# A gated attention and mixer kernel: where the last two chunks of the first z are loaded

## The chip, the cores and the metric

The kernel runs on one core of a Trainium2 chip. The metric is the device time of one execution, in microseconds (us). Seven inputs are read from HBM, one output is written to it; the time covers all of that.

The core's engines each run their own list of instructions in order: TensorE (PE in the profile, PEld for its weight loads), VectorE (DVE), ScalarE (ACT), GpSimd (POOL) and SyncE (SP). An instruction that has to wait for another engine or for a DMA holds up all that stands behind it on its own engine. SyncE, ScalarE and GpSimd can issue DMAs, each on a queue of its own (q1, q10 and q0 in the profile).

## The reference

Batch 8, sequence S = 3008, width D = 256, z of width 64, all float32. First a gated attention, then an MLP mixer on what it gives:

```python
scores = scale * np.matmul(z, z.transpose(0, 2, 1))      # scale = 1 / S
attn = np.maximum(scores, 0.0) ** 2
x = u * np.matmul(attn, v)
# mixer, for each batch
xt = x.transpose(0, 2, 1)
h = np.maximum(xt @ w_tok1, 0.0) @ w_tok2                # over the sequence, 256 channels
u = x + h.transpose(0, 2, 1)
h2 = np.maximum(u @ w_ch1, 0.0) @ w_ch2                  # over the width, 1536 channels
out = u + h2
```

The scores of a batch are a product of z with itself, so z is needed transposed (width on the partitions), both as weights and as the moving side.

## The kernel before

The sequence is cut in six chunks of 512 rows (the last has 448); a chunk is four tiles of 128 rows. For each batch the kernel goes over six blocks of queries (one chunk each), and within a block over the six chunks of keys. For a pair of chunks TensorE makes scores in two units (two key tiles each, line 440), ScalarE applies the ReLU and the scale (line 478), VectorE squares (line 486), and TensorE multiplies with v and accumulates (line 593 in the very first block, line 677 in the others). VectorE then multiplies with the transposed u (line 835). When a batch's blocks are done, its mixer is mixed in between the attention of the following batch.

Nearly everything is ordered at build time. The code carries a small planner: it holds an estimate of when each engine is free, when each tile is ready, and what each step costs, and picks the next piece for TensorE from that (`while cur[0] is not None or heads or tails`). The order so found is then fixed in each engine's list of instructions. On the chip, semaphores decide when each instruction really starts. An estimated due time therefore changes the order, not the waiting.

The start of the program is written out by hand, and the change is in it. The z of batch 0 isn't transposed like the others':

- `first_z(c)` loads chunk c of the first z in float32 into a tile `zf` (line 162). Chunk 5 has three full tiles and a half one; the half one is filled by two more loads of the same 64 last rows (line 165), to both halves of the partitions. Even chunks go over SyncE's queue, odd ones over ScalarE's, and the two loads of last rows one over each.
- `double_first_z(c)` has VectorE cast a chunk to bfloat16 and write it twice side by side (line 171), as `zr`.
- `turn_on_pe` transposes it on TensorE against an identity matrix (line 177); a copy moves the result to `zT` (by ScalarE, line 1639, for chunks 0 and 1; by VectorE, line 1643, for chunk 3, and line 1573 for chunks 4 and 5). Chunk 2 alone is transposed by a DMA on SyncE's queue (`turn_first_z`, line 149).
- Chunks 4 and 5 are handled by `late_z(c, landed)`: it asks the planner for a cast on VectorE at the time `landed`, an urgent piece on TensorE when that cast is done, and a copy on VectorE behind it.

Around this, GpSimd issues the first chunk of v at once (line 211, `load_v(0, 0)`). Its other five chunks of the first v, and then u, come behind `after(...)`, a small copy that waits for ScalarE's copy of chunk 1's transpose. TensorE begins with seven filler products (line 198) and fills up to the first product with v with five more. The tile pool gives VectorE's `zr` and GpSimd's v their buffers.

In the first block the keys are taken in the order 0, 1, 3, 2, 4, 5, so the scores of chunks 4 and 5 are made last.

The wait of the casts, on VectorE, is on the semaphores of the loads: the cast of chunk 5 waits for its own load and for both loads of last rows. On VectorE the squares that follow stand behind such a cast.

Of the kernel before, what the change touches and what calls it, by code (L numbers as in the profile page):

```python
# [15 lines left out]
GK = 4  # L16
# [41 lines left out]
def kernel(  # L58
# [11 lines left out]
    nc = tc.nc  # L70
# [11 lines left out]
    NG = KT // GK  # L82
# [30 lines left out]
    def rows_of(ap, c):  # L113

        n = full_tiles[c]
        return ap[c * QW:c * QW + n * P, :].rearrange("(p t) d -> p t d", t=n)

    def last_rows(ap):
        return ap[(KT - 1) * P:, :]
# [27 lines left out]
    def turn_first_z(c):  # L147

        nc.sync.dma_start_transpose(
            out=zTs[0][:, c * GK:c * GK + GK, :],  # L150
            in_=double_first_z(c).rearrange("p t h d -> p (t h d)"))
# [5 lines left out]
    def first_z(c):  # L157

        zf = sb.tile([P, GK, d_qk], F32, tag="v", name="zf", bufs=ROOM["v"])
        n = full_tiles[c]  # L160
        queues = [nc.sync, nc.scalar]
        queues[c % 2].dma_start(out=zf[:, :n, :], in_=rows_of(z[0], c))
        if n < GK:
            for r in range(2):
                queues[r].dma_start(
                    out=zf[r * TAIL:(r + 1) * TAIL, n, :], in_=last_rows(z[0]))
        return zf

    def double_first_z(c):
        zr = sb.tile([P, GK, 2, d_qk], BF16, tag="xT", name="zr0", bufs=ROOM["xT"])  # L170
        nc.vector.tensor_copy(zr[:], zf0[c].unsqueeze(2).to_broadcast([P, GK, 2, d_qk]))
        return zr

    def turn_on_pe(zr, zp):

        for t in range(GK):
            nc.tensor.matmul(  # L177
                zp[:, t, :], zr[:, t].rearrange("p h d -> p (h d)"), ident[:],
                start=(t == 0), stop=True, skip_group_check=True)

    def bank_pair(slot, name):

        if slot == RING and not last_psum:
            first.close()
            last_psum.append(ctx.enter_context(
                tc.tile_pool(name="last_psum", bufs=1, space=bass.MemoryType.PSUM)))
        pool = psum if slot < RING else last_psum[0]
        return pool.tile([P, 2, QW], F32, tag=f"ps{slot}", name=name, bufs=1)
# [12 lines left out]
    def load_v(b, c):  # L201
        if b == 0:

            vt = sb.tile([P, GK, D], BF16, tag="fl", name="v_sb", bufs=ROOM["fl"])
            live["fl"] += 1
            fl_free.pop(0)
        else:
            vt = sb.tile([P, GK, D], BF16, tag="v", name="v_sb", bufs=ROOM["v"])
            live["v"] += 1
        n = full_tiles[c]  # L210
        nc.gpsimd.dma_start(out=vt[:, :n, :], in_=rows_of(v[b], c))
        if n < GK:
            for r in range(2):
                nc.gpsimd.dma_start(
                    out=vt[r * TAIL:(r + 1) * TAIL, n, :], in_=last_rows(v[b]))
        vs[b, c] = vt
        v_in[b, c] = Done(pe[0] + 9.0 if b > 1 else 0.0)
        loading(LOAD)
# [120 lines left out]
    def push(engine, ready, busy, lat, fn, first=0, room=(), done=None, frees=()):  # L339
        op = Op(ready, busy, lat, fn, first, room, done, frees)  # L340
        waiting[engine].append(op)
        return op.done
# [80 lines left out]
    def score_run(us, start):  # L423
        for unit in us:
            (b, q, g), pr = unit
            zT = zTs[b].rearrange("p t s -> p (t s)")
            W = widths[q]
            slot, free_at = take_slot()
            begin = max(start, free_at, known(turned[b, q], turned[b, g]))
            cost = column_time(W)  # L430
            if triangle(b, q, g):

                cost = (column_time(QW), column_time(P))[pr]
            begin, start = on_pe(begin, "half", cost)
            sc = bank_pair(slot, "sc")
            for r, i, c0, c1 in parts(unit):
                k = z_tile(b, r, g * GK + i) * P
                m = z_tile(b, r, q * GK) * P
                h = slice(r * d_qk, (r + 1) * d_qk)
                nc.tensor.matmul(  # L440
                    sc[:, r, c0:c1], zT[h, k:k + P], zT[h, m + c0:m + c1],
                    start=True, stop=True)
            if pr == 0:
                live["at"] += 1
                at_free.pop(0)
            busy = 0.92
            if triangle(b, q, g):
                busy = (0.87, 0.43)[pr]
            if grain(b, q, g) < GK and pr == 0:
                early[b, q, g] = [Done() for _ in range(GK)]  # L450
            done = push("act", begin + cost + 0.21, busy, busy + 0.16,
                        lambda t, unit=unit, sc=sc: relu(unit, sc, t))
            ring.append((done, slot))
# [424 lines left out]
    def take_slot():  # L878
        slot = min((s for s in ring if s[0].t is not None), key=lambda s: s[0].t)
        ring.remove(slot)  # L880
        return slot[1], slot[0].t
# [576 lines left out]
    zero = sb.tile([P, QW], BF16, tag="xT", name="zero", bufs=ROOM["xT"])  # L1458
    nc.vector.memset(zero[:], 0.0)
    make_identity(nc, ident)  # L1460
    zf0 = [first_z(c) for c in range(NG)]
    load_v(0, 0)
    nc.gpsimd.memset(zs[:, 0, :], 0.0)
    nc.gpsimd.memset(zs[:, KT + 1, :], 0.0)
# [96 lines left out]
    def late_z(c, landed):  # L1561


        zr = []

        def turn(end):
            slot, _ = take_slot()
            zp = bank_pair(slot, "zp")[:, 0, :].rearrange("p (t s) -> p t s", s=P)
            turn_on_pe(zr[0], zp)
            turned[0, c] = Done()  # L1570
            ring.append((push(
                "dve", end + 0.2, 0.66, 0.8,
                lambda t: nc.vector.tensor_copy(zTs[0][:, c * GK:c * GK + GK, :], zp),
                first=1, done=turned[0, c]), slot))

        cast = push("dve", landed, 0.42, 0.55, lambda t: zr.append(double_first_z(c)))
        heads.append(Piece(0.23, [cast], turn, urgent=True))


    def first_u(landed):  # L1580

        ur = urs.pop((0, 0))

        def turn(end):
            slot, _ = take_slot()
            up = bank_pair(slot, "up").rearrange("p r (t s) -> p (r t) s", s=P)
            for i in range(QW // P * DT):
                t, h = divmod(i, DT)
                nc.tensor.matmul(  # L1589
                    up[:, i, :], ur[:, t, h * P:(h + 1) * P], ident[:],  # L1590
                    start=(i % 4 == 0), stop=True, skip_group_check=True)
            ring.append((push("dve", end + 0.2, 1.15, 1.3, lambda t: evacuate(up)), slot))

        def evacuate(up):
            uTs[0, 0] = sb.tile([P, QW // P, DT, P], BF16, tag="uT", name="uT", bufs=3)
            nc.vector.tensor_copy(
                uTs[0, 0].rearrange("p t h s -> p (t h) s"), up)

        heads.append(Piece(0.45, [Done(landed)], turn, urgent=True))
# [36 lines left out]
    for c in range(DT):  # L1636
        zp = first_acc(c).rearrange("p (t s) -> p t s", s=P)
        turn_on_pe(double_first_z(c), zp)
        nc.scalar.copy(zTs[0][:, c * GK:c * GK + GK, :], zp)
    turn_first_z(2)  # L1640
    zp = bank_pair(2, "zp")[:, 0, :].rearrange("p (t s) -> p t s", s=P)
    turn_on_pe(double_first_z(3), zp)
    nc.vector.tensor_copy(zTs[0][:, 3 * GK:4 * GK, :], zp)
# [8 lines left out]
    pe[0] = 5.3  # L1652
    free.update(act=5.75, dve=5.0, sp=7.0)
    score_run(units[:2], 5.3)
    late_z(4, 7.8)
    late_z(5, 9.0)
    first_u(18.5)

    goals = {(1, 1): (0, 1 + HALF)}
# [147 lines left out]
```

## Time and profile before

| | us |
|---|---|
| median of 3 runs (1116.61 to 1116.9) | 1116.72 |
| the profiled execution: its time | 1117.16 |
| its span, first to last instruction | 1115.0 |
| TensorE busy in the span | 1104.5 |
| VectorE busy | 761.9 |
| ScalarE busy | 673.0 |
| GpSimd busy | 152.2 |
| TensorE busy from 8.70 to 30 us (21.30) | 21.09 |
| TensorE busy from 30 to 60 us (30.00) | 30.00 |
| ScalarE busy from 30 to 60 us (30.00) | 28.97 |

The granted clock of TensorE is 0.999 of full speed. The times of a trace are counted from its first instruction. A busy TensorE isn't TensorE at its peak, since the ends of pipelined products are modelled; that it never stands idle in a stretch is read from the waits and from the chain. The chain of waits is followed back from the last instruction: at each step to what released it, or to the instruction before it on its engine. A line of a DMA gives its tiles, the queue that issued it, its size and the time from issue to landing. In a timeline the columns are start, duration, engine, line, operation and tiles; "x3" merges three that follow each other, and the bracket behind tells how long the engine was idle before, and what ended that.

### The profile page before, as it was taken

The numbers are of one execution on the slowest core, as the hardware profiler recorded it, in microseconds if no ns is written. First come the engines' busy times: TensorE is split into PE (matmuls) and PEld (weight loads), VectorE is DVE, ScalarE is ACT, GpSimd is POOL, SyncE is SP. The second block draws the span as 40 slices with busy tenths as digits, with TensorE's granted clock in tenths as the row PEclk, the third lists the DMA queues.
The fourth block names the chain that finished last, engine by engine and source line by source line (L and its number), as shares of the span: only waits on it lengthen the run. The fifth ranks groups of instructions, "written<-read, shape, count | busy, mean of one in ns | idle before, by whom it ended". The sixth has DMA issues, their size and how long they took to land.

```text
span 1115.0 us, 26448 instructions
## 1 busy us (share of the span) xinstructions
PE 1104.5 (99%) x10714; PEld 666.6 (60%) x10788; DVE 761.9 (68%) x1587; ACT 673.0 (60%) x840; POOL 152.2 (14%) x387
## 2 busy tenths in 40 slices
PE   9999999999999999999999999999999999999998
PEld 3555654666447665676545765567654576545676
DVE  7887875676756867568656676566756677655676
ACT  8997585545755467555665456664666636743464
POOL 5401000221002210022100221003210021000000
PEclk9999999999999999999999999999999999999999
DMA  9999485997859988598694997869888697574222
GB/s 173 189 167 185 105 165 110 189 172 145 165 117 193 168 132 183 95 210 168 139 179 96 204 155 153 164 104 219 141 156 153 127 200 145 120 153 84 66 65 80
DMA packets 470411, 165.38 MB, mean 148 GB/s; under 512 B 433232, under 2 KB 448912, under 8 KB 470288
## 3 DMA queue, kind: packets, MB, share of 16 engines
q1 hardware_dynamic: 442432, 130.98, 59.2%
q0 software_dynamic: 27344, 32.32, 20.7%
q8 instruction: 84, 1.38, 0.5%
q14 instruction: 39, 0.32, 0.1%
q10 hardware_dynamic: 512, 0.38, 0.1%
HBM read 65.40 MB, written 24.64 MB: 81 GB/s over the span
## 4 chain that ended last, share of the span: by engine, by line
PE 98%; DMA 1%; issue 0%; POOL 0%; DVE 0%; ACT 0%; POOLq 0%
PE acc L677 42%; PE hp L977 22%; PE f L1096 18%; PE sc L440 6%; PE a_ps L900 4%; PE h_ps L927 4%; PE f L1209 1%; PE first_acc L593 1%; DMA v_sb<-in_v_dram 1%; PE op L1255 0%; PE zp L177 0%; PE up L1589 0%; DVE res L1287 0%; ACT a_sb L909 0%; POOL ident masks.py:199 0%
## 5 line engine op out<-in xcount | busy, mean ns | idle before, releaser
L1024 ACT ACTIVATE h2pre<-hp 128x1024 bf16<-128x1024 f32 (+1 forms) x287 | 283.3, 1005 | 226.6 <-PE hp L977 217.3
L677 PEld LDWEIGHTS <-v_sb 64*128 64x128 bf16 x4418 | 231.2, 94 | 227.8 <-issue 0.9
L677 PE MATMUL acc<-at,v_sb 64*128 64x512 bf16 (+1 forms) x2738 | 337.7, 374 | 0.0
L478 ACT ACTIVATE at<-sc 128x1024 bf16<-128x1024 f32 (+1 forms) x290 | 285.6, 1029 | 69.3 <-PE sc L440 64.1
L486 DVE TENSOR_TENSOR at<-at 128x1024 bf16<-128x1024 bf16 (+1 forms) x290 | 198.0, 686 | 123.5 <-ACT at L478 121.5
L977 PE MATMUL hp<-xT,w_ch_sb 128*128 128x512 bf16 (+1 forms) x1090 | 278.4, 374 | 3.3
L1096 PEld LDWEIGHTS <-h2pre 128*128 128x128 bf16 x3654 | 225.0, 98 | 55.3 <-issue 2.6
L677 PE MATMUL acc<-fl,v_sb 64*128 64x512 bf16 (+1 forms) x1680 | 191.8, 367 | 0.0
L1096 PE MATMUL f<-w_sums,h2pre 128*128 128x128 bf16 x2088 | 184.4, 219 | 0.1
L977 PEld LDWEIGHTS <-w_ch_sb 128*128 128x128 bf16 x1152 | 104.3, 98 | 82.1 <-issue 0.8
L440 PE MATMUL sc<-zT 64*128 64x512 bf16 (+1 forms) x732 | 131.3, 359 | 0.0
L1096 PE MATMUL f<-w_ch_sb,h2pre 128*128 128x128 bf16 x1566 | 128.5, 219 | 0.0
L811 DVE TENSOR_TENSOR cp<-acc,cp 128x512 f32<-128x512 f32 (+1 forms) x94 | 63.5, 675 | 57.1 <-ACT cp L805 56.3
L805 ACT COPY cp<-acc 128x512 f32<-128x512 f32 (+1 forms) x91 | 53.0, 582 | 80.7 <-PE acc L677 80.2
L466 ACT ACTIVATE at<-sc 128x512 bf16<-128x512 f32 (+3 forms) x152 | 54.8, 450 | 36.1 <-PE sc L440 34.0
L1049 DVE TENSOR_TENSOR h2pre<-h2pre 128x512 bf16<-128x512 bf16 (+1 forms) x141 | 56.3, 399 | 18.6 <-PE f L1096 17.7
L1170 DVE TENSOR_TENSOR res<-f,res 128x512 f32<-128x512 f32 (+1 forms) x47 | 30.6, 651 | 49.7 <-PE f L1096 49.7
L440 PEld LDWEIGHTS <-zT 64*128 64x128 bf16 x732 | 39.6, 94 | 41.6 <-issue 3.1
L1051 DVE TENSOR_TENSOR h2pre<-h2pre 128x512 bf16<-128x512 bf16 (+1 forms) x141 | 57.1, 405 | 9.4 <-PE hp L977 0.5
L936 DVE TENSOR_TENSOR xT<-xT,h_ps 128x1024 bf16<-128x1024 bf16 (+1 forms) x48 | 55.8, 1171 | 11.2 <-PE h_ps L927 11.2
L835 DVE TENSOR_TENSOR xT<-cp,uT 128x512 bf16<-128x512 f32 (+1 forms) x94 | 62.4, 664 | 1.2
L1052 DVE TENSOR_TENSOR h2pre<-h2pre 128x512 bf16<-128x512 bf16 (+1 forms) x141 | 57.4, 407 | 4.3
(80 smaller groups left out, 603.0 us busy)
## 6 DMA issues: line engine op xcount, KB each, us to landing
out_dram<-res SPq DMA_DIRECT2D x80, 256.0 KB, 2.5
v_sb<-in_v_dram POOLq DMA_DIRECT2D x40, 256.0 KB, 4.8
ur<-in_u_dram POOLq DMA_DIRECT2D x40, 256.0 KB, 5.4
out_dram<-res SPq DMA_DIRECT2D x24, 128.0 KB, 2.1
w_tok_sb<-in_moe_w_tok_dram POOLq DMA_DIRECT2D x10, 256.0 KB, 10.2
zs<-in_z_dram POOLq DMA_DIRECT2D x35, 64.0 KB, 4.0
at<-at SPq DMA_TRANSPOSE x114, 2.4
fl<-at SPq DMA_TRANSPOSE x105, 4.5
```

The lines of the kernel that those rows point to most:

```text
L440: nc.tensor.matmul(sc[:, r, c0:c1], zT[h, k:k + P], zT[h, m + c0:m + c1], start=True, stop=True)
L478: nc.scalar.activation(view, sv, ACT.Relu, scale=inv_S)
L486: nc.vector.tensor_mul(view, view, view)
L677: nc.tensor.matmul(o, vs[blk.b, g][rows, i, dh * P:(dh + 1) * P], rhs, start=(dh, h) not in blk.begun, stop=stop, skip_group_check=True)
L811: nc.vector.tensor_add(cp[:, :W], acc[:, 0, :W], cp[:, :W])
L835: nc.vector.tensor_mul(xT[:, dh, :full * P].rearrange("p (t s) -> p t s", s=P), acc[:, :full * P].rearrange("p (t s) -> p t s", s=P), uT[: ...
L977: nc.tensor.matmul(hp[:, r, :W], w_ch1_sb[:, dc, cc * P:(cc + 1) * P], xT[:, dc, :W], start=(dc == 0), stop=(dc == DT - 1))
L1024: nc.scalar.activation(h2[:, :, :W], hp[:, :, :W], ACT.Relu)
L1049: (3, lambda: nc.vector.tensor_sub(a11, a11, a21)),
L1051: (2, lambda: nc.vector.tensor_sub(a22, a22, a11)),
L1052: (4, lambda: nc.vector.tensor_sub(a12, a12, a22))]
L1096: banked(nc.tensor.matmul(to[:, j, :], lhs[:, j * P:(j + 1) * P], rhs, start=m in (1, 2) and c2 == 0 and j == 0, stop=c2 == CHT // 2 - 1, ...
```

## The change

The chunks 4 and 5 of the first z are no longer loaded with the other four, but once the transpose of chunk 2 has been issued, and both over SyncE's queue; the two loads of last rows go there too. The due times that the planner is given for their casts are later.

```diff
@@ first_z
         n = full_tiles[c]
-        queues = [nc.sync, nc.scalar]
+        queues = [nc.sync, nc.scalar] if c < GK else [nc.sync, nc.sync]
         queues[c % 2].dma_start(out=zf[:, :n, :], in_=rows_of(z[0], c))
         if n < GK:
             for r in range(2):
@@ the start
     make_identity(nc, ident)
-    zf0 = [first_z(c) for c in range(NG)]
+    zf0 = [first_z(c) for c in range(GK)]
     load_v(0, 0)
@@ the first transposes
     turn_first_z(2)
+    zf0 += [first_z(c) for c in range(GK, NG)]
     zp = bank_pair(2, "zp")[:, 0, :].rearrange("p (t s) -> p t s", s=P)
     turn_on_pe(double_first_z(3), zp)
@@ before the planner's loop
     score_run(units[:2], 5.3)
-    late_z(4, 7.8)
-    late_z(5, 9.0)
+    late_z(4, 9.0)
+    late_z(5, 10.5)
     first_u(18.5)
```

GK is 4 and NG is 6. Since the due times are the planner's, the order of the first 60 us on TensorE, VectorE and ScalarE differs from the one before; GpSimd's order doesn't. SyncE's list begins, built, as follows (left before, right changed):

```
before                                    changed
load z chunk 0                            load z chunk 0
load z chunk 2                            load z chunk 2
load z chunk 4                            transpose of chunk 2 (waits for its cast)
load last rows                            load z chunk 4
transpose of chunk 2 (waits for its cast) load z chunk 5
transpose of u ...               load last rows
                                          load last rows
                                          transpose of u ...
```

On ScalarE the loads of chunk 5 and of the last rows, which stood between the load of chunk 3 and the table load, are gone.

## The prediction

> **What bounds the kernel now.** I read the chain of waits over the whole span first, then TensorE's waits, then the chain between 8 and 25 us, where the change acts.
>
> ```profile
> PE 98%; DMA 1%; issue 0%; POOL 0%; DVE 0%; ACT 0%; POOLq 0%
> PE wp L198 <- DVE zero L1459: 1.2, 1, 1.2
> PE first_acc L593 <- DMA v_sb<-in_v_dram: 0.9, 1, 0.9
> PE zp L177 <- DVE zr L171: 0.3, 1, 0.3
> PE first_acc L593 <- issue: 0.2, 1, 0.2
> ```
>
> TensorE is 98% of the chain, and these four waits are all it has: 2.6 us. The chain first meets TensorE when the first chunk of v lands:
>
> ```profile
> 1.44 7.21 DMA v_sb<-in_v_dram
> 8.65 0.05 issue
> 8.70 1.04 PE first_acc L593 x4
> 9.73 0.22 PE zp L177 x4
> 9.96 0.32 PE sc L440 x2
> 14.91 1.83 PE first_acc L593 x8
> ```
>
> From 8.70 us on nothing is idle on TensorE, so each us that it waits after that is added to the time, and at most what it idles before 8.70 can be won. The columns are start, duration, work. Two prices stand here: a 512-column product costs 0.216 us (1.83 for eight, less 0.10), and each change between full products (v, transposes) and half ones (scores) about 0.10 (the 0.32 for a score pair that takes 0.22 elsewhere).
>
> Next, the loads that move, what they feed, and what SyncE does:
>
> ```profile
> 0.74 1.35 SPq L162 DMA_DIRECT2D zf<-in_z_dram  x3
> 2.14 0.58 SPq L165 DMA_DIRECT2D zf<-in_z_dram  x1
> 4.70 1.31 SPq L149 DMA_TRANSPOSE zT<-zr  x1
> zf<-in_z_dram SPq DMA_DIRECT2D x1, 128.0 KB, 2.5
> zf<-in_z_dram ACTq DMA_DIRECT2D x1, 96.0 KB, 8.2
> zf<-in_z_dram SPq DMA_DIRECT2D x1, 16.0 KB, 8.3
> zT<-zr SPq DMA_TRANSPOSE x1, 5.9
> 5.84 2.74 POOL L211 DMA_DIRECT2D v_sb<-in_v_dram  x5
> 8.03 0.43 DVE L171 CAST zr<-zf 128x512 bf16<-128x512 f32 x1 [0.45 <-DMA zf<-in_z_dram]
> 10.60 0.42 DVE L171 CAST zr<-zf 128x512 bf16<-128x512 f32 x1
> ```
>
> The last number of a DMA line is us from issue to landing. Chunk 4 is cast at 8.03, chunk 5 (with its two loads of 64 last rows) at 10.60; both are there when TensorE wants them. Five loads of v, 1.2 MB, are issued from 5.84.
>
> **The change, part by part.**
> Removed: chunk 4 and one load of last rows from SyncE's front (0.45 + 0.58 us of issue), chunk 5 and the other from ScalarE's (0.46 + 0.55). On SyncE this hides behind its wait for the cast until 4.70; on ScalarE behind its wait for TensorE until 4.58. Worth nothing there. What can gain is the first v load: it shares the DMA engines with 256 KB less. Bound: TensorE's idle 0.86 us before 8.70; a loss has no reason.
>
> Moved: four issues behind the transpose of chunk 2 on one queue. SyncE issues the transpose at 4.70 as before, since that waits for chunk 2's cast, then chunk 4 at 6.01, chunk 5 at 6.46, last rows at 6.91 and 7.49. Behind them on SyncE stands the transpose of u, issued at 19.91 before and waiting for u, so that queue hides it. GpSimd issues the same order.
>
> When does the last of them land (call it T)? Bounds: quiet, as the first chunk, 2.5 us: 7.49 + 2.5 = 10.0. As the last rows did: 7.49 + 8.3 = 15.8. The nearest row is how the queues share when GpSimd loads and SyncE transposes run together, for instance from 31 to 32 us:
>
> ```profile
> q0 software_dynamic: 101, 0.17, 92.3%
> q1 hardware_dynamic: 102, 0.03, 18.5%
> ```
>
> Packets for packet: GpSimd's queue (q0) and SyncE's (q1) alternate, some 102 a us each, though SyncE's are small. The moved loads are 128 + 128 + 64 + 64 = 384 packets (one a partition row), so 384 / 102 = 3.8 us beside GpSimd's loads. They start when the transpose ahead of them is through: it landed at 4.70 + 5.9 = 10.6; chunk 4 and one set of last rows, 192 packets, no longer stand before it, and from 6 to 8 us SyncE's queue moved 574 packets in 2 us, so 0.7 us sooner, 9.9. T = 13.7. These packets carry up to 1 KB where the row's carry 256 B; by bytes, 0.26 MB of z and 384 x 2 KB of v at the 200 GB/s of that window are 5.2 us, T = 15.1. I take 14.0, nearer the packet count.
>
> [...]
>
> Added wait: VectorE's cast of chunk 5 waits for T. In the changed kernel's built order VectorE does three squares, cast 4, a square, cast 5, copy of chunk 4's transpose, a square, copy of chunk 5's, squares; before, cast 4 stood after the first square. TensorE does six v products, two score pairs, two v products, transposes of chunk 4, two v products, a score pair, two v products, transposes of chunk 5. With the 8.70 start that is 6 x 0.216 + (0.44 + 0.10) + (0.43 + 0.10) + 0.22 + 0.43 + 0.32 + 0.53 = 3.86 us: TensorE stands at chunk 5's transposes at 12.56. They can start at T + 0.42 (cast) + 0.08 (two hand-overs, of about 0.05 as at 8.65) = 14.5. Stall: 1.94 us. An earlier v only lengthens this wait, so the gain of up to 0.86 is eaten. What is queued behind cast 5: copy, square, copy, square (0.69 and 0.64 us each) end at 15.2, 15.8, 16.5, 17.2; TensorE wants the first at about 15.6 and the copy of chunk 5 at about 16.6, so no second stall, with margins of a few tenths.
>
> Due times 9.0 and 10.5 instead of 7.8 and 9.0 also change the order up to about 60 us; counts of products and of the five fillers are equal. Scores stand more scattered: nine runs of scores instead of seven in the first block, two more, each with two mode changes: 4 x 0.10 = 0.4 us. After 60 us TensorE's order is the same.
>
> Sum: 0 + 1.94 + 0.4 = +2.3 us. The profiled execution took 1117.16 (span 1115.0, the rest lies outside it), so it would take 1119.5 and the span 1117.3; the median is 0.44 lower: 1116.72 + 2.3 = **1119.1**.
>
> **The rivals.**
> *Loads hidden, v sooner (not slower).* The moved packets slip through before the v loads fill the engines: GpSimd's first was issued at 5.84, the last rows at 7.49. For it: SyncE's queue ran 287 packets a us from 6 to 8. Against: from 8 to 10 us it moved 76 packets in all. It decides if T is below 12.06; then the time is +0.4 less up to 0.86: 1116.3 to 1117.1.
>
> *A partly hidden load.* T between 12.06 and 13.85: +0.4 to +2.2, 1117.1 to 1118.9. The row for it is the transposes of u, 5.8 us from issue under load: 7.49 + 5.8 = 13.3, +1.6, 1118.3.
>
> *The queue starves.* One transpose that SyncE issued at 25.80 landed at 42.25, 16.5 us later, beside GpSimd's loads. Its 1024 packets against 384 scale to 6.2 us, but behind 512 of the transpose at 102 a us from 6.0 all 896 end at 14.8 at the soonest; with 2 us more until the first packet moves, T = 16.8 and +5.1: 1121.8. ScalarE would then be short too; it is busy 28.97 of the 30 us after 30.
>
> *The change does nothing:* the built order has all four loads behind the transpose, so no.
>
> **How the numbers follow.** Under 0.2% (2.23 us) I count as no change, about what a measurement here can tell. Forecast, T from 13.85 to 15.8: 0.45. Starved: 0.10. Partly hidden: 0.22. Hidden: 0.19. Faster by over 2.23 us: 0.04, since only 0.86 us of idling is in reach. So slower 0.55, same 0.41, faster 0.04. The likeliest case alone spans 1118.9 to 1120.8; the range for 8 in 10 takes in nearly all hidden and partly hidden cases and leaves out most of the starved one: 1116.5 to 1121.0.
>
> **What would show it.** Right: the last z load lands near 14, VectorE's cast of chunk 5 starts there after some 3 us of waiting for a DMA, TensorE waits some 2 us for that cast before line 177, and the lag persists unchanged to the end. Wrong: cast 5 before 12 us (rival one); TensorE waiting for something else, such as the second v chunk (landed 10.95, and slower if z packets take its turns), or new gaps between 20 and 60 us, which would make the order and not the load the cause. A first v product at about 7.9 shows that the first v gained.

## The result, and the profile after

| | before | changed |
|---|---|---|
| median of 22 executions each, us | 1116.92 | 1121.18 |
| ratio, 95% interval | | 1.0052 (1.0030 to 1.0074) |
| profiled execution: time, us | 1117.16 | 1120.24 |
| its span, us | 1115.0 | 1118.1 |
| its mean granted clock | 0.999 | 0.998 |

The change made the kernel slower, by 4.3 us in the medians. Forecast were 1119.1 us and a range up to 1121.0, so the time lies just outside it. One thing is needed to read the numbers: most versions, the old one too, have executions of 1123 to 1138 us beside their usual ones, and where two of those lose their time is shown further down. Below 1123 us the old kernel's median is 1116.73 (93 of 109 executions in all comparisons) and the changed one's 1121.03 (22 of 34). Below, "usual" means these.

First TensorE's waits over the whole span of the changed kernel, but for the 1.2 us at its start (engine, line, releaser; us in all, times, longest):

```profile
PE zp L177 <- DVE zr L171: 1.6, 1, 1.6
PE sc L440 <- DVE zT L1573: 0.2, 1, 0.2
```

The 0.9 us for v is gone, and so is the 0.3 for the first transposes; in their place TensorE waits 1.6 us for VectorE's cast at line 171. The chain of waits tells what that cast waited for (start, duration, work):

```profile
5.67 0.57 SPq L162
6.28 0.43 SPq L162
6.75 0.59 SPq L165
7.39 5.74 DMA zf<-in_z_dram
13.15 0.43 DVE zr L171
...
14.23 0.39 PE sc L440 x2
...
16.45 0.96 PE sc L440 x3
17.42 2.57 PE first_acc L593 x8
```

The second load of last rows is issued at 7.39 and lands 5.74 us later, at 13.13. The cast of chunk 5 starts at 13.15. Note the last two lines: eight v products take 2.57 us here, and 1.83 in the chain of before. The timeline shows the same from the engines' side (start, duration, engine, line, operation, tiles, then the idle time before):

```profile
7.74 1.47 PE L593 MATMUL first_acc<-at,v_sb 128*128 128x512 bf16 x6
9.40 0.42 DVE L171 CAST zr<-zf 128x512 bf16<-128x512 f32 x1
11.42 0.60 PE L593 MATMUL first_acc<-at,v_sb 128*128 128x512 bf16 x2
13.15 0.43 DVE L171 CAST zr<-zf 128x512 bf16<-128x512 f32 x1 [2.74 <-DMA zf<-in_z_dram]
13.64 0.40 PE L177 MATMUL zp<-ident,zr 128*128 128x128 bf16 x4 [1.62 <-DVE zr L171]
```

The first v product starts at 7.74 instead of 8.70: the first chunk of v lands 5.1 us after its issue instead of 7.2, and TensorE is busy until 7.74 with what stands ahead of that product. Not all of this is the change's doing, since in `e1_due` below, where the loads stand as before, that product starts at 8.28. Chunk 4 is in time; chunk 5 holds VectorE for 2.74 us and TensorE, idle from 12.02, for 1.62. The four moved loads as DMA issues (size of one, us from issue to landing):

```profile
zf<-in_z_dram SPq DMA_DIRECT2D x1, 128.0 KB, 2.8
zf<-in_z_dram SPq DMA_DIRECT2D x1, 96.0 KB, 4.4
zf<-in_z_dram SPq DMA_DIRECT2D x1, 16.0 KB, 5.2
zf<-in_z_dram SPq DMA_DIRECT2D x1, 16.0 KB, 5.7
```

The smaller the load and the later its issue, the longer it took: the bytes did not decide. Chunk 5 itself was there at 10.7. The two loads of 16 KB made it late.

The stall explains 1.62 of the lost 3.1 us and the early v takes 0.96 off. The rest is in the clock column of a table of short stretches (stretch, its length, busy time and instruction count of TensorE, weight loads, VectorE, ScalarE, GpSimd, then the granted clock):

```profile
12.00:13.00 1.00, 0.02 (x1) 0.00 (x0) 0.00 (x0) 0.55 (x1) 0.53 (x1) 1.00 1.15 208
15.50:16.00 0.50, 0.50 (x2) 0.04 (x2) 0.50 (x2) 0.50 (x2) 0.24 (x1) 0.50 1.10 209
16.00:17.00 1.00, 1.00 (x6) 0.13 (x4) 1.00 (x2) 0.60 (x1) 1.00 (x3) 0.50 1.10 205
18.00:19.00 1.00, 1.00 (x4) 0.35 (x3) 0.69 (x1) 0.97 (x2) 0.36 (x1) 0.57 1.09 195
30.00:60.00 30.00, 30.00 (x282) 14.31 (x278) 25.83 (x41) 29.34 (x34) 12.38 (x21) 1.00 1.19 192
```

From 15.45 to 18.87 us (0.95 of full in the half us before 15.5, 0.57 in the last us) TensorE ran at half its clock, though it was busy all that time. Two v products take 0.96 us in that stretch and 0.54 just before it, at 14.63, by the chain. Those 3.41 us at half the clock cost, as an estimate, half their length, 1.7 us. In the profile of before all of 15 to 19 us shows 1.00, for instance:

```profile
16.00:17.00 1.00, 1.00 (x8) 0.25 (x6) 0.78 (x2) 1.00 (x2) 1.00 (x2) 1.00 1.08 201
```

So of the 3.1 us by which the span grew, 1.62 + 0.2 - 0.96 + 1.7 = 2.6 are found. The order adds about 0.2 by two runs below (the prediction had 0.4); some 0.3 us have no place here. The two profiled executions are also nearer to each other than the usual medians, which differ by 4.3: that of before took 0.4 us more than its usual median, that of the changed kernel 0.8 less.

### The profile page after: what moved, and what is told of

Same layout as the page of the kernel before. It is cut to its first block, busy times and chain, and to the rows that moved or that the text cites. A ratio compares the mean times of both kernels' runs of the same rounds, so it can differ in the third digit from the quotient of the medians.

```text
span 1118.1 us, 26525 instructions
## 1 busy us (share of the span) xinstructions
PE 1110.9 (99%) x10788; PEld 665.0 (59%) x10788; DVE 760.8 (68%) x1586; ACT 673.8 (60%) x841; POOL 152.1 (14%) x387
## 4 chain that ended last, share of the span: by engine, by line
PE 98%; DMA 1%; SPq 0%; DVE 0%; issue 0%; ACTq 0%
PE acc L677 42%; PE hp L977 22%; PE f L1096 18%; PE sc L440 6%; PE a_ps L900 4%; PE h_ps L927 4%; PE f L1209 1%; PE first_acc L593 1%; DMA zf<-in_z_dram 1%; PE op L1255 0%; SPq L162 0%; DVE zr L171 0%; DVE zT L1573 0%; SPq L165 0%; SPq L149 0%
## 5 line engine op out<-in xcount | busy, mean ns | idle before, releaser
L977 PE MATMUL hp<-xT,w_ch_sb 128*128 128x512 bf16 (+1 forms) x1152 | 281.7, 375 | 0.0
```

What stands on the lines that cost most here:

```text
L977: nc.tensor.matmul(hp[:, r, :W], w_ch1_sb[:, dc, cc * P:(cc + 1) * P], xT[:, dc, :W], start=(dc == 0), stop=(dc == DT - 1))
```

## The experiments

Each is compared by its usual executions with 1116.73 for the old kernel and 1121.03 for the changed one. Where a kernel has added lines, its line numbers are shifted (593 is 600 in some).

### The order alone, and the placement alone

`e1_due` is the old kernel with the changed due times:

```diff
-    late_z(4, 7.8)
-    late_z(5, 9.0)
+    late_z(4, 9.0)
+    late_z(5, 10.5)
```

> The loads stand as before, only the due times are those of the change, so the order of the instructions on TensorE, VectorE and ScalarE is the changed kernel's. Theory (the load that lands late, and the half clock that its wait leaves behind, are the cost): no wait of TensorE for the cast of chunk 5, no half clock near 15 us, time within 0.5 us of before (116.9 above 1000, so 1116.5 to 1117.4). Rival (the new order is the cost, by scattered scores and more changes of mode): 1118 or more, with no wait for the cast.

Its usual executions, 4 of 12, have a median of 1116.73; the other eight took 1125.3 to 1131.2. From its timeline, a usual execution:

```profile
8.28 1.46 PE L593 MATMUL first_acc<-at,v_sb 128*128 128x512 bf16 x6
10.66 0.42 DVE L171 CAST zr<-zf 128x512 bf16<-128x512 f32 x1
```

Chunk 5 is cast at 10.66; TensorE waits for no cast, and its clock stays full (1.00 in all of 0 to 60 us). The first v product started 0.42 us earlier than in the profile of before, and the span, 1114.8 us, is 0.2 shorter: so the new order costs about 0.2 us, not the 0.4 of the prediction. `e3_rows_early` below, with the same order, says the same: 0.96 earlier, and a span 0.8 shorter (1114.2).

`e2_place` is the changed kernel with the old due times:

```diff
-    late_z(4, 9.0)
-    late_z(5, 10.5)
+    late_z(4, 7.8)
+    late_z(5, 9.0)
```

> The loads stand as in the change, the due times and so the order are those of before. Theory of the late load: still 2 to 5 us slower than before, 1119 to 1122, with TensorE waiting 1 to 3 us for the cast of chunk 5 and most likely a stretch of half clock after it. Rival (the order is the cost): back at 1116.5 to 1117.4.

1119.79, all 11 executions usual, ratio 1.0016 (0.9990 to 1.0042). The placement of the loads, not the order, brings the stall, as TensorE's waits show (the last rows landed at 13.85):

```profile
PE zp L177 <- DVE zr L171: 1.6, 1, 1.6
PE sc L440 <- DVE zT L1573: 0.5, 1, 0.5
```

And in the table of stretches, with the clock in the same column as above:

```profile
8.70:30.00 21.30, 18.82 (x120) 7.25 (x121) 16.24 (x26) 17.55 (x19) 12.60 (x24) 1.00 1.19 192
```

TensorE idles longer than in the changed kernel (1.6 and 0.5 us), yet its clock stays at 1.00 from 8.7 to 30 us, and the kernel is 1.2 us faster. The half clock that was expected here did not come in this execution; three of the eleven have a mean clock of 0.998 or 0.997 and took 1120.24 to 1121.88. The idle time alone is not what the changed kernel lost.

### Which of the moved loads

`e3_rows_early` puts the two loads of last rows ahead of the transpose again, one on each queue, and leaves both chunks behind it:

```diff
+    first_ends()                    # both loads of last rows, SyncE and ScalarE
     load_v(0, 0)
 ...
     turn_first_z(2)
     zf0 += [first_z(c) for c in range(GK, NG)]      # chunks 4 and 5, no last rows
 ...
```

> As the change, but the two small loads of the last rows are issued ahead of the transpose, one on SyncE's queue, one on ScalarE's; chunks 4 and 5 themselves stay behind it. Theory (the last thing to land sets the wait, and that is the last rows, at 13.1 us, while chunk 5 itself landed near 10.7): the cast of chunk 5 is free by about 11, TensorE waits less than 0.3 us for it, no half clock, and the sooner first v (first product with v at 7.7 instead of 8.7) is kept in part: 1116.0 to 1117.0. Rival (any z load behind the transpose is late, whatever its size): cast near 13, 1119 to 1121.

Usual median 1116.94 (7 of 12; the others 1128 to 1137), the old time: chunk 5 landed at 10.53 and its cast ran at 10.55 without a wait of TensorE. 32 KB of the moved 256 KB are the whole stall. The sooner first v (7.74) shows in the profiled execution, 1116.35, but not in the median.

`e8_only5_late` leaves only chunk 5 behind the transpose, and takes the old due times:

```diff
-        queues = [nc.sync, nc.scalar] if c < GK else [nc.sync, nc.sync]
+        queues = [nc.sync, nc.scalar] if c < LAST else [nc.sync, nc.sync]
 ...
+    first_ends()
 ...
-    zf0 += [first_z(c) for c in range(GK, NG)]
+    zf0.append(first_z(LAST))
```

> The order and due times of before; chunk 4 and the last rows are loaded ahead of the transpose, the last rows over both queues, and chunk 5 alone (96 KB) behind it. Theory: chunk 5 lands by 10, ahead of its cast at 10.6 in the kernel before; the first v has 96 KB less beside it and lands up to 0.5 us sooner; shorter group at 1116.2 to 1116.9. Rival (any z behind the transpose costs): 1118 or more.

Usual median 1116.72 (8 of 12). The chain has the load, but with nothing lost behind it:

```profile
5.90 5.03 DMA zf<-in_z_dram
10.93 0.02 issue
10.95 0.43 DVE zr L178
```

Chunk 5 landed at 10.93, later than the 10 that was expected and than the cast in the old kernel (10.60), but TensorE doesn't wait for its cast, and only 0.2 us for the copy behind it. The time is the expected one, with chunk 5 not ahead of its cast but just soon enough. One of the twelve executions took 1807.12 us with a mean clock of 0.602; it wasn't traced, and stays unexplained.

### What makes them late

`e5_v_held` is the changed kernel in which GpSimd issues the second chunk of v and then waits for the last rows before it issues the other four loads of v:

```diff
         if c == FIRST[1]:
+            after(zf0[LAST][:, full_tiles[LAST], :1])
```

> As the change, but GpSimd issues only one more load of v before the last rows of z have landed; the other four and u come behind. Theory (the moved loads are late because their packets take turns with the five v loads): the last rows land at 9.8 to 11 instead of 13.1, TensorE waits less than 0.3 us for the cast of chunk 5, no half clock near 15 us, main group of executions at 1116.0 to 1117.5, unless the held v chunks are late in their turn (then a wait for v_sb shows). Rival (the issues themselves, at 5.7 to 8.0 us on one queue, are the delay): the last rows still land near 13, 1119 to 1121.

1118.03, twelve usual executions of twelve, ratio 0.9992 (0.9964 to 1.0021). From its chain:

```profile
7.70 3.04 DMA zf<-in_z_dram
10.74 0.03 POOLq L123
```

And TensorE's waits:

```profile
PE first_acc L593 <- DMA v_sb<-in_v_dram: 0.8, 1, 0.8
PE sc L440 <- DVE cp L811: 0.7, 1, 0.7
```

The same 16 KB that took 5.74 us take 3.04 with one load of v beside them instead of five, though they are issued no sooner. The wait for the cast is gone, and the kernel is 3.0 us faster than the changed one. It is still 1.3 us above the old one: v is late in turn, for 0.8 us, and the wait of 0.7, at 79 us, is for a transpose of u, at the place where the long executions wait (below).

`e6_two_queues` gives chunk 5 and one load of last rows back to ScalarE's queue, at the new place:

```diff
-        queues = [nc.sync, nc.scalar] if c < GK else [nc.sync, nc.sync]
+        queues = [nc.sync, nc.scalar]
```

> As the change, in the same order on TensorE and VectorE, but chunk 5 and one load of last rows are issued on ScalarE's queue, behind its two copies, so that the four loads have two queues again. Theory (a queue's turns beside GpSimd's packets set the landing): half the packets on each queue, the last landing at 10.5 to 11.8; ScalarE's first ReLU moves from 5.9 to about 7.0, which costs up to 1 us at the first product with v; 1116.7 to 1118.3. [...]

Usual median 1117.58 (9 of 12; the others 1129 to 1132), ratio 1.0017 (0.9975 to 1.0059). From its timeline, the loads of the two queues and the cast of chunk 5:

```profile
5.26 0.33 ACTq L162 DMA_DIRECT2D zf<-in_z_dram  x1
5.63 0.70 ACTq L165 DMA_DIRECT2D zf<-in_z_dram  x1
5.81 0.57 SPq L162 DMA_DIRECT2D zf<-in_z_dram  x1
6.42 0.66 SPq L165 DMA_DIRECT2D zf<-in_z_dram  x1
11.95 0.43 DVE L171 CAST zr<-zf 128x512 bf16<-128x512 f32 x1
```

The last load is issued at 6.42 instead of 7.39, and the cast starts at 11.95 instead of 13.15; TensorE waits 0.6 us for it. Of the 1.2 us won, 1.0 is the earlier issue; from issue to cast it is 5.5 us against 5.8. So on SyncE's queue, though half the packets were gone from it, little was won beyond the issue time. The landing, 11.86, is a little later than the 10.5 to 11.8 of the theory, and the time lies in its range; that the time from issue fell by only 0.3 us speaks against the theory, by one execution of each kernel. The two loads on ScalarE's queue, issued first, landed at 8.44 and 9.59. The prediction held the number of a queue's turns to matter; here they mattered by that 0.3 us at most. The wait beside the v loads, 5.74 us against 3.04 in `e5_v_held`, comes on top of the issue time.

### The clock

`e4_fill7` is the changed kernel with seven products of zeros ahead of the transposes of chunk 5, into a bank that they overwrite:

```diff
 ...
+            if c == LAST:
+                fill(7, bank)
 ...
```

> As the change, with seven products of zeros (7 x 0.216 = 1.5 us) on TensorE ahead of the transposes of chunk 5, where it waits 1.6 us; they write a bank that the transposes overwrite. Theory (the wait leaves a half clock of 3.4 us behind, worth 1.7 us): the wait for the cast stays but is filled, the granted clock stays at 1.0 from 15 to 19 us, and the time falls by 1.2 to 2.2 us from the change's 1121, to 1118.5 to 1119.8. Rival (the lower clock is no consequence of the idle time, or isn't paid for): the same as the change, 1120.2 to 1121.5, or slower by the fillers.

Usual median 1119.55 (5 of 12; the others 1130 to 1138), 1.5 us below the changed kernel. The load is no sooner than in the changed kernel (landed at 14.19), but the products fill most of the wait, as TensorE's timeline shows:

```profile
10.97 0.40 PE L177 MATMUL zp<-ident,zr 128*128 128x128 bf16 x4 [0.94 <-DVE zr L171]
12.49 1.67 PE L198 MATMUL zp<-zero 128*128 128x512 bf16 x7
14.69 0.40 PE L177 MATMUL zp<-ident,zr 128*128 128x128 bf16 x4 [0.53 <-DVE zr L171]
```

In this execution chunk 4 was late too (0.94 us); of the wait for chunk 5, 0.53 is left idle. And the clock stays full, 1.00:

```profile
8.70:30.00 21.30, 19.44 (x123) 7.41 (x125) 14.82 (x24) 16.68 (x18) 11.97 (x23) 1.00 1.16 188
```

So the half clock is worth about 1.5 us, near the 1.7 estimated above, and it comes with the idling: with the gap filled it is gone from all five usual executions (mean clock 0.999 or 1.000). The executions of the changed kernel agree: of its 22 usual ones, 19 have a mean clock of 0.998 or 0.997, which is what 3.41 us at half clock make of 1118 (1 - 1.7 / 1118 = 0.998), and take 1120.24 to 1122.68. The other three, at 0.999 or 1.000, took 1118.88, 1119.49 and 1120.34: 2.2 to 3.6 us above the old kernel, where the prediction had 2.3.

Why `e2_place` escaped can be estimated from the records of the clock. That of the changed kernel's trace begins at 5.21 us; it has full clock for 10.240 us, half for 3.413, full for 1099.092, and half again behind the last product. These are 3, 1 and 322 periods of 3.4133. That of the trace of before begins at 4.15 us and has full clock for 1109.332 us, 325 such periods, and then half. So in both the clock changed at whole periods from the record's beginning, whose place is not the same in the two. One such period of the changed kernel runs from 12.04 to 15.45 and holds both waits, 1.8 us of 3.41. In `e2_place` the clock falls at the end of the run at 1116.03:

```profile
1116.00:1116.50 0.50, 0.00 (x0) 0.00 (x0) 0.00 (x0) 0.00 (x0) 0.00 (x0) 0.53 0.00 0
```

Full clock for 0.03 of that half us. If the periods run through here as in the other two, 323 of them earlier lies 13.52, in the middle of its stall (12.74 to 14.36). TensorE's busy time in the period of the changed kernel (first line) and in the two of `e2_place` that share the stall:

```profile
12.04:15.45 3.41, 1.61 (x11) 0.65 (x12) 2.30 (x5) 1.30 (x2) 1.58 (x3) 1.00 1.17 205
10.11:13.52 3.41, 2.48 (x13) 0.76 (x12) 0.97 (x2) 3.14 (x4) 1.43 (x3) 1.00 1.14 209
13.52:16.94 3.42, 1.93 (x12) 0.79 (x14) 3.07 (x6) 1.32 (x2) 2.15 (x4) 1.00 1.17 205
```

So 1.8 us of idling in one period, against 0.9 and 1.5. The longest wait is 1.6 us in both, so it is not the length of one wait that differs, but how much of it falls into one period; that this decides is my reading, and no run tests it alone. In the traces of before and of the changed kernel the clock fell behind the three periods with the most idling, 1.8 us here and 2.5 and 3.4 at the two ends, and behind no other; the idlest of those has 0.86. It fell behind periods with 2.2 us idle in `after_again`, 2.4 in `e9_weights_8` and 2.6 in `look_e1`. Between the 1.5 of `e2_place`, which rests on the estimated place of its periods, and 1.8 us nothing was measured.

`after_again` is the changed kernel itself once more.

> The changed kernel once more, beside the other kernels of this call. Theory: two groups of executions; the shorter one at 1118.8 to 1122.7 with a median near 1121, and in it the mean clock tells the time: at 0.999 to 1.000 (no half clock after the wait) 1118.8 to 1120, at 0.997 to 0.998 above 1120. Rival (the clock has no part): no relation between the two.

Median of 12 executions 1121.49, ratio 1.0065 (1.0025 to 1.0106). Of the seven usual ones, that with a mean clock of 0.999 took 1119.49, the six with 0.998 took 1120.84 to 1121.57, as expected. The traced one (1120.91) shows the same stall, 2.2 us long with the last rows landing at 13.48, and the same half clock (0.50 from 16 to 18 us). Its span is 3.8 us above that of before.

### The long executions

`look_e1` is the kernel `e1_due`, run once for a profile:

> A look for the trace of an execution of the longer group (1125 to 1131 us, mean clock 0.994 to 0.997), which 8 of 12 executions of this kernel fell in. Theory A (TensorE's clock comes up late at the start, or falls again within the first 60 us, since idle pieces fall into its windows of 3.41 us): stretches of half clock in the first 60 us, some 10 us or more in all, and no wait of TensorE for z. Theory B (the clock falls somewhere later, without idle time): half clock in the middle of the run.

It happened to be a long one, 1131.77. It lost its time far from the change. VectorE's timeline has the place:

```profile
89.19 0.69 DVE L835 TENSOR_TENSOR xT<-cp,uT 128x512 bf16<-128x512 f32 x1 [13.37 <-DMA uT<-ur]
```

The chain tells what it waited for, and the table of stretches what it cost TensorE:

```profile
60.98 28.12 DMA uT<-ur
```

```profile
60.00:100.00 40.00, 27.45 (x252) 14.79 (x250) 20.62 (x34) 23.29 (x28) 4.09 (x7) 0.83 1.42 114
```

A transpose of u on SyncE's queue lands 28.12 us after its issue, at 89.1, and TensorE, behind VectorE, idles 12.5 us, in which its clock falls (0.81 of full from 80 to 81 us), and then runs at a lower clock for some us more (0.86 from 94 to 95). In the usual execution of the same kernel the same transpose took 15.2 us and landed at 75.3. Between 60 and 75 us GpSimd's queue carries weights and u beside it, and those are as late: a median of 25.6 us to landing for the four weight loads, 28.9 for u (15.4 and 17.3 in the usual execution). The delay begins well before that: the first load of weights, at 33 us, took 15.4 us instead of 10.7. That the two queues hold each other up is my reading; no run here separates them. Neither theory names a wait at this place, so both missed.

`look_e4`, the kernel `e4_fill7` once for a profile:

> The same look for the changed kernel with seven products of zeros in its wait, of which 7 of 12 executions took 1130 us and more. Theory A: half clock in the first 60 us. Theory B: half clock later on.

1131.45, with the same wait: 11.1 us of TensorE for the copy of line 811 behind that transpose. These two executions show where the time is lost in them, and nothing on the start.

`e9_weights_8` asks for the weights less densely, in the kernel `e1_due`:

```diff
-    W_LATER = 4
+    W_LATER = 8
```

> As e1_due, but the loads of the weights on GpSimd are spread over 32 steps instead of 28, so they come a little later each; the order after 50 us changes a little with it. Theory (the longer group is SyncE's transpose of the u of block 4, which takes turns with GpSimd's weight loads and lands at 89 us instead of 75): fewer packets beside it, so the longer group shrinks from 8 of 12 to 3 of 12 or fewer. Rival (the longer group comes from something else): 6 of 12 or more stay above 1125.

Eight of 12 executions were still long (1123.2 to 1131.8, usual median 1117.13), six of them above 1125, and its profiled one (1124.16) has the wait too, 5.8 us. The long executions became no fewer, which the rival had expected, though the wait is at the same place. Eight long ones of 12 in `e1_due`, seven in `e4_fill7`, five in `e3_rows_early`, four in `e8_only5_late` with the one of 1807.12, three in `e6_two_queues`, none of 23 in `e2_place` and `e5_v_held`, 12 of 34 in the changed kernel and 16 of 109 in the old one: the frequency depends on the version, and what sets it is open. It is no part of the 4.3 us between the usual executions, but it widens the ratio.

## Why the prediction was wrong

Point by point:

- "then chunk 4 at 6.01, chunk 5 at 6.46, last rows at 6.91 and 7.49": the queue's order held, issues 0.1 to 0.3 us earlier.
- T, the landing of the last row, forecast 14.0: 13.13, and 13.48 to 14.19 in the three other traces of usual executions that have all four loads on SyncE's queue behind the transpose and all v loads beside them. Neither the quiet bound (10.0) nor the starving one (16.8) came. The way there was wrong twice, and that the number is near is in part luck: the transpose of chunk 2 landed at 7.2, not near 10, and chunk 4 at 8.5; from 7.2 to the last row it then took 5.9 us, not 3.8. `e5_v_held` bears the cause out: with four of the five v loads held back, 10.74. `e6_two_queues` takes back one part of the argument: with two queues the last load took 5.5 us from issue to cast instead of 5.8, so a queue's turns mattered little there; the company of the v loads mattered much (3.04 us to landing in `e5_v_held` instead of 5.74).
- "An earlier v only lengthens this wait, so the gain of up to 0.86 is eaten": the v product started 0.96 earlier, a little more than the bound, since the wait of 0.3 before the first transposes went too. TensorE stood idle from 12.02; from the first v product to there it took 4.28 us, not 3.86.
- "Stall: 1.94 us" is reckoned from a first v product at 8.70. In the same terms it is 1.62 + 0.2 for the copy behind it - 0.96 = 0.9 us here, and 1.4 in the trace of `after_again` (2.2 + 0.2 - 0.96). A second stall was excluded with a margin of a few tenths, and there is almost none.
- Order, 0.4: about 0.2 by the spans of `e1_due` and `e3_rows_early`.
- "the lag persists unchanged to the end": TensorE is busy in all of 30 to 60 us, and there is no further wait.

The step that failed is in the first part: "each us that it waits after that is added to the time". It priced the stall at its own length. The waiting cost that, and then the 3.41 us at half clock that it set off, 1.7 us by the trace and 1.5 by `e4_fill7`. 1119.1 plus 1.5 to 1.7 is 1120.6 to 1120.8; the usual median is 1121.0. Without the half clock the changed kernel took 1118.88 to 1120.34 (three executions), and 1119.55 with the gap filled, so the rest of the forecast comes out near. That is in part luck: its stall and its order were too large in the traces, and the traces have some 0.3 us or more that no term here names.

The profile of before doesn't show this price: behind the first products its longest idle time was 0.86 us, at a full clock. But it has a sign that TensorE isn't always at full speed. The seven filler products of the start take 0.45 us each, twice the 0.216 of a product later on, in a stretch where the clock column reads 1.00, though that trace's record of the clock begins only at 4.15 us:

```profile
1.20 3.13 PE L198 MATMUL wp<-zero 128*128 128x512 bf16 x7 [1.20 <-DVE zero L1459]
```

So what a stall does to TensorE's speed was an unknown cost, and should have been bounded like the others. The range had no case for it: its upper end came from a later landing, and the starved case, whose 1121.8 lies near the measured time, was the wrong mechanism for it.

## What to carry to other kernels

Price a stall on TensorE twice: by its length, and by what its clock does afterwards. Here 1.8 us idle in a period of 3.41 brought 3.41 us of half clock, and in `e2_place` an estimated 1.5 didn't; seven products of zeros in the gap won 1.5 us, though the load stayed late. When loads move, look at the last and smallest of them: beside five loads of v, 16 KB took 5.7 us, twice the 2.8 of 128 KB issued ahead of it, and with the two small loads in front (`e3_rows_early`) the stall was gone, so here what was small and needed soon belonged ahead of the crowd. And when a ratio looks larger than the traces explain, list the single executions before looking for a cause near the change.

## What the runs showed of the hardware

- The granted clock fell to 0.50 for one period (15.45 to 18.87) after a period with 1.8 us of idling, and stayed at 1.00 in `e2_place`, whose 2.4 us of idling the estimated bound of a period cuts into 0.9 and 1.5.
- Of four loads in a row on one queue, beside the loads of v, the 128 KB one took 2.8 us from issue to landing and the last, of 16 KB, 5.7; with one load of v beside it instead of five the last took 3.04 (`e5_v_held`).
- The same transpose of u landed 15.2 us after its issue in a usual execution of `e1_due` and 28.12 us in a long one of the same kernel.
